# First products on row halves: seven products for eight in weighted groups 2 to 5 of an attention and routing kernel

## The chip, the cores and the metric

The kernel runs on one core of a Trainium2 chip. The metric is the device time of one execution in microseconds; several runs are taken, and their median counts. All data are 32-bit floats.

## The reference, cut to what matters

A sketched attention makes `x`, 4352 tokens of 128 numbers. Eight experts of two layers then work on every token, and their results are added with weights `P` that come from a balancing (Sinkhorn) loop over the gate's logits:

```python
for e in range(E):                      # 8 experts
    h = np.maximum(x @ w1[e], 0.0)      # 128 -> 1024, "first product"
    ye = h @ w2[e]                      # 1024 -> 128, "second product"
    out += P[:, e:e + 1] * ye
```

The weights are positive, so a token may be weighted before its first product as well as after its second.

## The kernel before, in words

**Groups, items, blocks.** The tokens are worked on in groups (line 632 on). Eight plain groups do experts 0 and 1 while attention and routing still run; their results wait in the tiles `kept`. Then come the weighted groups: five with three tiles of 256 tokens each (starts 1280, 512, 2048, 2816, 3584; these are "weighted groups 1 to 5"; the second does experts 2 to 7, the others 1 to 7), and a sixth with two tiles of 256. A pair of group and expert is an item. An item of a three-tile group has two blocks (`blocks`, line 882); a block holds four pieces `f` of 128 of the 1024 hidden numbers.

**One block of a three-tile group.** `four` (line 956) issues eight steps. A step is one first product (`first`, line 910): 128 rows of `x` against 128 columns of W1, as two matmuls in two column tiles of 64, for 512 or 256 tokens, into a fresh bank of the pool `aps` (four banks). ScalarE then writes the Relu of the bank into the block's buffer (`hx` for even blocks, `hb` for odd ones). VectorE makes the sums of hidden blocks that a fast second product needs (`sums`, ten instructions of 512 or 256 columns on lines 980 and 1000, from Relu results). Eight steps later `twenty` (line 1063) has the second products: ten pairs, each one product in each column tile, 128 rows, 256 tokens, added up in the four banks `s0` to `s3` over all experts of the group. Their weights are 16 sums of W2's blocks (`sums_of_four`, line 226) and four blocks of W2 as they are. GpSimd makes the 16 sums in group 1 with ten instructions an expert (line 242), SP stores them in DRAM, and groups 2 to 5 load them (line 230).

**Tokens and weights.** `prepare_x` (line 680) loads an item's weights `P` with a broadcasting DMA (line 674) and GpSimd multiplies the tokens by them (line 678), one item ahead. `prepare_w` (line 655) has SP load W1 and W2. `weigh_kept` (line 694) weighs the kept results of experts 0 and 1 on GpSimd.

**A group's end.** When a bank has its last product, `part_of_twenty` (line 814) copies it out on ScalarE and queues some 23 sums and 5 copies on half the partitions; then three transposes and the stores follow (`put`, line 711). They are taken one by one from the list `later` while the next group runs.

**What sets the order.** `steps` (line 1117) issues everything in program order, and TensorE and VectorE keep that order. `tc.keep_in_program_order` does the same for single instructions of GpSimd and SP. Elsewhere the framework orders ScalarE's, GpSimd's and SP's instructions. The two-tile groups go through `two` and `seven`: blocks of two pieces `f`, four steps, and seven second products, the last of which uses only one column tile. Waits between engines come from the framework, by what an instruction reads and writes.

## Time and profile before

| | us |
|---|---|
| median of 3 runs (919.47 to 919.66) | 919.57 |
| span of the profiled execution | 917.7 |
| DVE busy from 650 to 700 us | 30.93 |
| ACT busy from 650 to 700 us | 20.66 |

The profiled execution's span runs from its first to its last instruction; its own time as a run isn't listed apart, so the median, 1.9 us more, stands for it. PE is TensorE's matmuls, PEld its weight loads, DVE VectorE, ACT ScalarE, POOL GpSimd, SP the engine that issues most DMAs. A line such as "L916 PE MATMUL a<-xe,w 128\*64 128x512 f32 x1088 | 336.3, 592" names the line of the code, the engine, what is written and read, the weights' rows and columns, the result's partitions and columns, how many instructions there are, their busy time together and the mean time of one in ns. A product of 32-bit floats stands there as two matmuls, its two passes. A matmul's listed time includes a tail that the next one overlaps, so its rate is read from starts. In the table by stretches each line gives the stretch, its length, and the busy time and count of PE, PEld, DVE, ACT and POOL, then TensorE's granted clock, the DMA engines' busy share and GB/s. A square bracket in a timeline names what the engine waited for.

### The profile page before, as it was taken

What the parts mean: (1) busy time and instruction counts of PE and PEld (TensorE: products, weight loads), DVE (VectorE), ACT (ScalarE), POOL (GpSimd) and SP (SyncE); (2) the same over time, 40 slices, a digit from 0 to 9 for tenths busy, and PEclk for the clock granted to TensorE, in tenths of its full rate; (3) what the DMA queues carried; (4) which work ended last, traced back from release to release, by engine and by line L of the source; (5) the groups of instructions that cost most, each with busy time, mean ns of one, the idle gap of its engine ahead of it and who ended that gap; (6) DMA issues with size and microseconds to landing.
All of it is one profiled execution on the core that took longest, in us unless ns stands there. A gap on an engine that the chain in (4) does not pass through costs nothing.

```text
span 917.7 us, 18881 instructions
## 1 busy us (share of the span) xinstructions
PE 910.4 (99%) x7434; PEld 695.8 (76%) x7434; DVE 687.7 (75%) x1173; ACT 422.7 (46%) x918; POOL 210.4 (23%) x212
## 2 busy tenths in 40 slices
PE   9999999999999999999999999999999999999997
PEld 6777544466666688888888888888888888888997
DVE  7678699888876798766975666966667987678654
ACT  3355465554444454444544444544445444446443
POOL 3121100175545422200210011110100352340110
PEclk9999999999999999999999999999999999999999
DMA  9994100213445545534364343463434556552550
GB/s 250 307 276 165 54 1 1 70 64 110 161 142 152 172 133 158 182 110 146 115 173 148 110 150 110 122 200 120 140 113 165 148 161 190 164 192 92 150 158 13
DMA packets 91305, 128.15 MB, mean 140 GB/s; under 512 B 25392, under 2 KB 69504, under 8 KB 86480
## 3 DMA queue, kind: packets, MB, share of 16 engines
q1 hardware_dynamic: 88384, 121.42, 43.0%
q0 software_dynamic: 1600, 5.36, 2.0%
q8 instruction: 58, 0.95, 0.4%
q10 hardware_dynamic: 1232, 0.16, 0.1%
q14 instruction: 31, 0.25, 0.1%
HBM read 107.88 MB, written 19.05 MB: 138 GB/s over the span
## 4 chain that ended last, share of the span: by engine, by line
PE 96%; DVE 2%; ACT 1%; DMA 1%; issue 0%; SPq 0%; DVEq 0%; ACTq 0%
PE a L916 51%; PE s L1107 41%; PE a L347 1%; PE a L462 1%; DMA kx<-in_k_dram 1%; DVE hb L933 1%; PE a L314 0%; PE s L376 0%; PE a L426 0%; PE s L392 0%; DVE cs L602 0%; PE a L496 0%; PE a L392 0%; ACT hb L920 0%; DVE rs L596 0%
## 5 line engine op out<-in xcount | busy, mean ns | idle before, releaser
L916 PE MATMUL a<-xe,w 128*64 128x256 f32 (+1 forms) x2560 | 615.4, 470 | 0.0
L916 PEld LDWEIGHTS a<-xe,w 128*64 128x64 f32 x2560 | 306.3, 137 | 39.2 <-issue 1.6
L920 ACT ACTIVATE hb<-a 128x256 f32<-128x256 f32 (+4 forms) x408 | 195.1, 480 | 241.7 <-PE a L916 210.9
L1107 PE MATMUL s<-hb,ws 128*64 128x256 f32 (+3 forms) x1312 | 276.4, 395 | 0.2 <-DVE hb L933 0.2
L920 ACT ACTIVATE hx<-a 128x256 f32<-128x256 f32 (+1 forms) x360 | 167.3, 465 | 211.6 <-PE a L916 194.6
L1107 PE MATMUL s<-hx,ws 128*64 128x256 f32 x1280 | 253.6, 379 | 0.0
L1107 PEld LDWEIGHTS s<-hb,ws 128*64 128x64 f32 x1312 | 161.5, 137 | 67.9 <-issue 14.7
L980 DVE TENSOR_TENSOR hb<-hb 128x512 f32<-128x512 f32 (+1 forms) x204 | 138.3, 687 | 97.9 <-ACT hb L920 93.8
L678 POOL TENSOR_TENSOR xe<-xT,xe 128x768 f32<-128x768 f32 (+2 forms) x41 | 84.0, 2050 | 490.5 <-DMA xe<-pT 363.6
L1107 PEld LDWEIGHTS s<-hx,ws 128*64 128x64 f32 x1280 | 159.6, 137 | 48.3
L980 DVE TENSOR_TENSOR hx<-hx 128x512 f32<-128x512 f32 (+1 forms) x204 | 149.0, 741 | 59.1 <-ACT hx L920 54.1
L1107 PE MATMUL s<-hb,w 128*64 128x256 f32 (+3 forms) x536 | 120.3, 408 | 0.0
L916 PE MATMUL a<-xT,w 128*64 128x416 f32 (+3 forms) x512 | 119.9, 462 | 0.0
L1107 PE MATMUL s<-hx,w 128*64 128x256 f32 x384 | 81.8, 379 | 0.0
L933 DVE TENSOR_TENSOR hb<-hb 128x416 f32<-128x416 f32 (+7 forms) x84 | 59.9, 713 | 19.4 <-ACT hb L920 15.8
L1107 PEld LDWEIGHTS s<-hb,w 128*64 128x64 f32 x536 | 60.0, 137 | 17.4 <-issue 6.5
L916 PEld LDWEIGHTS a<-xT,w 128*64 128x64 f32 x512 | 49.5, 137 | 25.0 <-issue 15.6
L242 POOL TENSOR_TENSOR ws<-w 128x256 f32<-128x256 f32 (+1 forms) x70 | 61.1, 907 | 8.1 <-DMA w<-in_moe_w_dram 8.0
L933 DVE TENSOR_TENSOR hx<-hx 128x256 f32<-128x256 f32 (+1 forms) x65 | 37.2, 576 | 25.4 <-ACT hx L920 24.2
L1107 PEld LDWEIGHTS s<-hx,w 128*64 128x64 f32 x384 | 46.4, 137 | 4.4
L980 DVE TENSOR_TENSOR pqg<-hb 128x512 f32<-128x512 f32 x68 | 43.2, 676 | 0.0
L980 DVE TENSOR_TENSOR pqg<-hx 128x512 f32<-128x512 f32 x68 | 37.7, 594 | 0.0
(180 smaller groups left out, 489.8 us busy)
## 6 DMA issues: line engine op xcount, KB each, us to landing
w<-in_moe_w_dram SPq DMA_DIRECT2D x82, 512.0 KB, 5.5
ws<-ws SPq DMA_DIRECT2D x34, 1024.0 KB, 4.9
xe<-pT SPq DMA_DIRECT2D x34, 384.0 KB, 4.0
ws<-ws SPq DMA_DIRECT2D x12, 512.0 KB, 3.1
ph<-qa SPq DMA_DIRECT2D x12, 288.0 KB, 4.8
rb<-qb SPq DMA_DIRECT2D x3, 1152.0 KB, 7.6
pb<-pT SPq DMA_DIRECT2D x6, 384.0 KB, 8.6
kx<-in_k_dram SPq DMA_DIRECT2D x4, 544.0 KB, 5.0
```

What stands on the lines that cost most here:

```text
L242: tc.keep_in_program_order(nc.gpsimd.tensor_tensor(ws[:, c:c + len(ns)], blocks(x), blocks(y), op=Alu.subtract if off else Alu.add))
L347: nc.tensor.matmul(pv[64 * s:64 * (s + 1), i], kp[0:n, H * t + h].rearrange("p i j -> p (i j)"), vx[0:n, slots[h], t, :], start=(t == 0 an ...
L462: nc.tensor.matmul(pn[64 * s:64 * (s + 1), t, 2 * i:2 * i + 2].rearrange("p h d -> p (h d)"), ph[:, i, s, 64 * t:64 * (t + 1)], kvs[b % 2] ...
L678: tc.keep_in_program_order(nc.gpsimd.tensor_tensor(out, x, pb, op=Alu.mult))
L916: nc.tensor.matmul(ph[sl], loaded_w[j][0][:, P * f + H2 * s:P * f + H2 * (s + 1)], sources[j][:, lo:hi], start=True, stop=True, tile_posit ...
L920: nc.scalar.activation(out=out, in_=ph, func=Act.Relu)
L933: nc.vector.tensor_tensor(out, a, b, op=Alu.subtract)
L980: nc.vector.tensor_tensor(out if not isinstance(out, tuple) else places(*out), places(*a), places(*b) if isinstance(b, tuple) else b, op=A ...
L1107: nc.tensor.matmul(sums[g][i][H2 * s:H2 * (s + 1), n * place:n * (place + 1)], w, x, start=c == 1 and not seeded, stop=c == per, tile_posi ...
```

## The change

Weighted groups 2 to 5 get a new routine, `middle`, with an order of its own, and group 1 prepares what it needs.

- **The first product.** W1 and the tokens are cut in pieces: rows 0 to 63 and 64 to 127, and tokens 0 to 383 and 384 to 767 (`HALF` is 384). Two pieces `f` that lie two apart are taken together. A product of two by two blocks is then done with seven block products instead of eight, in Winograd's way: with sums of W1's pieces (`wf`, beside W1's own pieces in `wl`), and sums of the tokens' pieces (`de`, and the changed upper half of `xe`). Each of the seven is 64 rows, 128 columns (two column tiles) and 384 tokens; three or four in each half `p` of the block run in the upper 64 rows of the array and the others in the lower ones.
- **Sums of its results.** The four banks of `aps` become `bx`, `by`, `bb[0]` and `bb[1]`. In each half `p` of a block ScalarE copies product 1 from `bx` to `bb[p]` (`seed`), copies product 5 out (`m5`), and does four Relu of 384 columns; VectorE does two sums (`vector`) of a bank and the copied product 5, one of them into the bank `by`.
- **The second product** is cut into row halves as well, so that all matmuls have the same tiles: 20 pairs of 64 rows instead of 10 of 128. All 20 forms of W2 are now stored and loaded (16 before). Two row halves that add into the same bank are kept apart by waits: the second waits for an instruction of ScalarE or VectorE that saw a later first product (`witness`).
- **The tokens.** VectorE weighs half an item a block, ScalarE copies it, and four DMAs issued by GpSimd that add to their target make the token sums (`join_halves`).
- **W1's forms** are made once, in group 1 (`forms_of_first`): copies and sign changes by ScalarE, three adding DMAs an expert by GpSimd, stores by SP.
- **Group 6's** sums of W2 (`sums_of_two`) are made again by GpSimd instead of being loaded. `weigh_kept` goes in pieces of 256 columns.
- **Order.** Each instruction of a block has a time in a period of 8.83 us; the instructions are issued in the order of these times, blocks overlapping. At the start ten whole products of an older block are put in between, at the end three blocks of group 6.

```diff
+        def product(out, row, w, c0, x, start, stop):
+            r = ROWS[row]
+            for s in range(2):
+                sl = slice(H2 * s, H2 * (s + 1))
+                nc.tensor.matmul(out[sl], w[r, c0 + H2 * s:c0 + H2 * (s + 1)], x[r], start=start, stop=stop,
+                                 tile_position=(H2 * row, H2 * s), skip_group_check=True)
...
+            product(*{1: (bx, 0, w1, fa, xe[:, 0], True, False), 2: (bx, 1, w1, fa, xe[:, 0], False, True),
+                      3: (by, 1, w1, fb, de[:, 0], False, True), 4: (b, 1, wf, fb, xe[:, 1], False, True),
+                      5: (b, p, wf, fa, de[:, 1], True, False), 6: (b, 0, wf, fb, de[:, 0], False, True),
+                      7: (b, 0, w1, fb, xe[:, 1], False, True)}[n])
...
+        def scalar(k, p, what):
+            b = bb[p]
+            if what == "seed":
+                witness(k, p, 1, nc.scalar.copy(b, bx))
+            elif what == "m5":
+                witness(k, p, 5, nc.scalar.activation(out=m5s[p], in_=b, func=Act.Copy, scale=1.0 if p else -1.0))
+            else:
+                out, x = {"11": (raw(k, p, 0, 0), bx), "12": (raw(k, p, 1, 0), by), "21": (raw(k, p, 0, 1), b),
+                          "22": (raw(k, p, 1, 1), raw(k, p, 1, 1))}[what]
+                ins = nc.scalar.activation(out=out, in_=x, func=Act.Relu)
...
+        def vector(k, p, what):
+            ins = nc.vector.tensor_tensor(by if what == 1 else raw(k, p, 1, 1), bb[p], m5s[p], op=Alu.add)
...
+        FIRST = {1: (1.40, 5.39), 2: (3.85, 6.44), 3: (5.60, 10.11), 4: (6.61, 11.37), 5: (-0.07, 4.62), 6: (3.76, 6.34), 7: (5.60, 8.35)}
+        SCALAR = {"seed": (2.93, 5.41), "m5": (2.86, 5.40), "11": (4.03, 9.98), "12": (6.42, 11.91), "22": (11.16, 12.70), "21": (7.68, 12.16)}
+        VECTOR = {1: (5.46, 7.30), 2: (5.97, 8.48)}
+        SECOND = ((14.81, 12.90, 15.44, 15.42, 15.62, 19.89, 21.05, 20.44, 21.90, 22.30),
+                  (17.63, 17.59, 19.18, 21.80, 21.41, 23.38, 23.73, 22.41, 24.54, 24.29))
+        EASE, WEIGH = (11.93, 16.87, 13.85), 13.49
...
+        def second_product(k, i, row):
+            r = ROWS[row]
...
+                before = written.get((bank_, 1 - row))
+                op = None
+                if before is not None and bank_ not in waited[row]:
+                    op = next((op for seen, op in witnesses if seen > before), None)
...
+                mm = into(g, w[r], x[r], *place, row)
+                if op is not None:
+                    tc.add_manual_dep(mm.ins, op, SYNC, reason="row tiles of one bank")
...
+    SUMS = ((14.78, (U4, U2), (at(0, 0), at(3, 0)), (at(0, 1), at(3, 1)), False),
+            (11.17, (U1,), (at(3, 0),), (at(3, 2),), False), (13.68, (V4,), (U1,), (at(0, 2),), False),
+            (15.02, (V3, V1), (U4, U2), (at(1, 1), at(2, 1)), True),
+            (14.65, two_, (at(1, 1), at(3, 1)), (at(0, 1), at(2, 1)), True),
+            (16.68, pqg[:, 2], (V3,), (at(1, 0),), True),
+            (14.66, (BB, U3), (at(1, 2), at(2, 0)), (at(2, 2), at(2, 2)), False),
+            (19.10, (W1, W2), (V4, V4), two_, False), (16.15, (W3, V2), (BB, U3), (V1, at(1, 2)), False),
+            (20.68, (W4,), pqg[:, 2], (V2,), True))
...
+    def join_halves(j):
+
+        xe, de = sources[j]
+        for out, x in ((de[upper], xe[lower]), (de[lower, 1], xe[upper, 1]), (de[:, 0], de[:, 1]),
+                       (xe[lower, 1], xe[lower, 0])):
+            tc.keep_in_program_order(nc.gpsimd.dma_start(out=out, in_=x, accum_op=Alu.add))
...
+    def forms_of_first(e, w1):
...
+        def turn(out, x):
+            nc.scalar.activation(out=out, in_=x, func=Act.Copy, scale=-1.0)
+
+        def plus(out, x):
+            tc.keep_in_program_order(nc.gpsimd.dma_start(out=out, in_=x, accum_op=Alu.add))
...
+        def one():
+            nc.scalar.copy(d, w[:, :, 1])
+            turn(fa, w[:, :, 0])
+
+        def two_():
+            nc.scalar.copy(t3[lower], w[upper, :, 1])
+            turn(n12, w[lower, :, 1])
+            plus(a[:, 0:F // 2], a[:, F // 2:F])
+
+        def three():
+            turn(z[lower], w[upper, :, 1])
+            plus(b[lower, F // 2:F], less[lower])
+
+        def four_():
+            turn(z[upper], d[lower])
+            put_(wf[lower, :, 0], d[lower])
+            put_(wl[lower, :, 1], t3[lower])
+
+        def five():
+            plus(a[:, 0:F // 2], b[:, 0:F // 2])
+
+        def six():
+            put_(wf[upper, :, 0], z[upper])
+            put_(wf[:, :, 1], d)
+
+        return {2: one, 4: two_, 6: three, 8: four_, 12: five, 16: six}
...
+    PERIOD = 8.83
...
+        for n, i in enumerate((0, 1, 2, 5, 3, 4, 6, 7, 8, 9)):
+            add(0.2 + 0.8 * n, whole_product, ks[0] - 2, i)
```

The keys 2 to 16 of `forms_of_first` are steps of the item in group 1 (eight a block; 16 is the next item's first). In the tables the two numbers of `FIRST`, `SCALAR` and `VECTOR` are for the halves `p` = 0 and 1, the two rows of `SECOND` for the row halves, and `SUMS` lists VectorE's ten sums with their times.

More of the change, by code (lines that the diff above doesn't have):

```diff
@@ L185, with load_w @@
     load_q(0, 16)
-    def load_w(e, sums=True, again=False):
+    lower, upper = slice(0, H2), slice(H2, P)
+    def load_w(e, sums=True):
         w1 = wpool.tile([P, F], F32, tag="w1", name="w1")
@@ L571, in routing @@
     def routing():
+        for e in range(1, E):
+            raw_of_first(e)
         yield 5
@@ L625 @@
     engines = mybir.EngineType
-    lower, upper = slice(0, H2), slice(H2, P)
     NMAX = 512
@@ L835, in part_of_twenty @@
             do(y[lower, 1], y[lower, 1], own[1][lower, 1], True)
-        elif k == 3:
+        if all(i in own for i in range(4)):
             e0, e1, e2, e3 = (own[i] for i in range(4))
@@ L1098, in into @@
         seen = done[g]
-        c = seen[i, s] = seen.get((i, s), 0) + 1
-        per = len(es) * (FO // (4 if t == 3 else 2)) * TIMES[t][i][s]
+        c = seen[i, s] = seen.get((i, s), 0) + (2 if t == 3 and row is None else 1)
+        per = len(es) * (FO // (2 if t == 2 else 4)) * TIMES[t][i][s] * (2 if t == 3 else 1)
         if g in DIRECT:
@@ L1119, in steps, with between @@
         todo, sums_at, t = {}, {}, 0
-        for k in range(len(blocks) + 5):
+        ks = range(len(blocks) + 5)
+        news = [k for k in range(len(blocks)) if new_of(blocks[k][0])]
+        def between(t):
+            for do in sums_at.pop(t, ()):
+                do()
+            while soon:
+                soon.pop(0)()
+            for b, p in todo.pop(t, ()):
+                second(b, p)
+        for k in ks:
+            if k in news:
+                if k == news[0]:
+                    while todo or sums_at:
+                        between(t)
+                        t += 1
+                    with tc.manual_schedule(engines={engines.DVE, engines.PE, engines.Activation}):
+                        middle()
+                    yield 0
+                continue
             if k == len(blocks) - 2:
```

394 lines of the change are left out of this document (289 added, 105 removed).

## The prediction

> **What bounds the kernel now.** I read the page's busy shares first, then the chain that ended last, then the table by stretches of time.
>
> ```profile
> span 917.7 us, 18881 instructions
> PE 910.4 (99%) x7434; PEld 695.8 (76%) x7434; DVE 687.7 (75%) x1173; ACT 422.7 (46%) x918; POOL 210.4 (23%) x212
> PE 96%; DVE 2%; ACT 1%; DMA 1%; issue 0%; SPq 0%; DVEq 0%; ACTq 0%
> ```
>
> ```profile
> 250.00:300.00 50.00, 50.00 (x385) 33.20 (x383) 35.99 (x55) 20.68 (x43) 23.23 (x23) 1.00 0.49 151
> 650.00:700.00 50.00, 50.00 (x380) 40.34 (x378) 30.93 (x54) 20.66 (x43) 3.80 (x2) 1.00 0.44 140
> ```
>
> In both stretches of the weighted groups TensorE is busy 50.00 of 50.00 us at clock 1.00, and 96% of the chain lies on it. So a column less to stream is time won, until another engine becomes the bound. How long one column takes, and one block:
>
> ```profile
> 624.69 1.07 DVE L980 TENSOR_TENSOR hx<-hx 128x512 f32<-128x512 f32 x2 [0.71 <-ACT hx L920]
> 634.17 1.08 DVE L980 TENSOR_TENSOR hb<-hb 128x512 f32<-128x512 f32 x2 [0.71 <-ACT hb L920]
> ```
>
> ```profile
> 347.85 0.43 PE s L1107 x4
> 348.28 0.86 PE a L916 x4
> 349.14 0.43 PE s L1107 x4
> ```
>
> The first two lines (VectorE's timeline) are the first sum of two blocks that follow one another: a block takes 9.48 us. In the chain, four matmuls are one product in two column tiles, each in two passes: 0.43 us for 256 columns, 0.86 for 512, so 0.216 and 0.43 us a pass. A block has 4 first products of 512 columns, 4 of 256 and 10 pairs of second products of 256: 4 x 0.86 + 14 x 0.43 = 9.46 us. The block is TensorE's stream and nothing else.
>
> **The change, part by part.** *The stream of groups 2 to 5.* They hold 6 + 3 x 7 = 27 items of 2 blocks, 54 blocks. A first product on 128 rows becomes, in each half p of a block, seven products on 64 rows and 384 columns. Seven land in each row half of the array per block (p0: 5, 1, 6, 7 above, 2, 3, 4 below; p1: 1, 6, 7 above, 2, 3, 4, 5 below). The ten second products run once in each half. A tile then has 7 x 2 passes of 384 columns, 0.323 us each (between the rows for 256 and 512), and 20 of 0.216: 4.52 + 4.32 = 8.83 us. Against 9.48 that removes 0.645 us a block, **34.8 us** in 54.
>
> Do four tiles of 64 x 64 run at once? The trace has such tiles in the lower row half alone, never four. The nearest rows:
>
> ```profile
> 8.74 1.99 PE L376 MATMUL s<-qT,wq 64*128 64x512 f32 x8
> 10.66 2.33 PEld L347 LDWEIGHTS a<-v,kp 128*64 128x64 f32 x72 [0.76 <-PE s L376]
> 22.86 0.85 PE L376 MATMUL s<-qT,wq 64*128 64x288 f32 x4
> 23.65 0.65 PE L916 MATMUL a<-xT,w 128*64 128x256 f32 x4
> ```
>
> Eight passes of 512 columns in two row halves took 1.99 us; one after another would be 8 x 0.43 = 3.4. So row halves run side by side, as column halves do in every block. 72 weight loads, with as many matmuls among them, took 2.33 us: 32 ns a pair. The change issues 136 pairs a block, 65 ns each. I take full concurrency; the other end is two tiles at a time (a rival).
>
> And must a matmul wait for the one ahead of it in the program, though its tile is free? Around an odd product for one column tile (the seventh of `seven`):
>
> ```profile
> 863.51 0.38 PE L1107 MATMUL s<-hx,ws 128*64 128x256 f32 x1
> 863.65 0.38 PE L916 MATMUL a<-xe,w 128*64 128x256 f32 x1
> 863.73 0.38 PE L1107 MATMUL s<-hx,ws 128*64 128x256 f32 x1
> ```
>
> A product of the next step starts in the other tile between two passes of the odd one. A tile goes on by itself, at least one pass ahead. The Trainium skill (TensorE: Matmul & The Clock Gate, Part 3, The mechanism) says that matmuls start and end strictly in program order. By that rule the two passes of one tile would hold up the next tile, and two of four would run at a time (the rival's price); these rows speak against it.
>
> *VectorE.* It keeps its ten sums a block and gets four sums out of the banks and one weighing.
>
> ```profile
> 629.98 1.02 DVE L980 TENSOR_TENSOR pqg<-hx 128x512 f32<-128x512 f32 x2
> 630.91 0.69 DVE L980 TENSOR_TENSOR hx<-hx,pqg 128x512 f32<-128x512 f32 x1
> 631.52 1.48 DVE L980 TENSOR_TENSOR hx<-hx 128x512 f32<-128x512 f32 x2
> 636.11 0.42 DVE L980 TENSOR_TENSOR hb<-hb 128x256 f32<-128x256 f32 x1 [0.87 <-ACT hb L920]
> L477 DVE TENSOR_TENSOR rd<-a,rc 128x384 f32<-128x384 f32 x9 | 5.0, 558 | 0.3
> ```
>
> Back to back, 512 columns take 0.61 us from start to start (630.91 to 631.52) though each is listed with 0.69, and 512 with 256 behind it 0.93 (629.98 to 630.91), so 256 take 0.33. The last line is the nearest to the new sums, bank and tile, 384 columns: 0.558 listed, 0.47 by the same overlap. Sum: 6 x 0.61 + 4 x 0.33 + 5 x 0.47 = 7.3 us. To that come a finished group's 23 sums and 3 transposes, three pops a block over ten blocks: 0.9. **8.2 of 8.83 us**, or, if no overlap is had, 6 x 0.69 + 4 x 0.42 + 5 x 0.56 + 1.1 = 9.7. The order written out puts no sum behind the one that it needs, so I take the lower end; the upper is a rival.
>
> *The handoffs.* Product 7 waits for the sum v1, product 4 for v2; in between VectorE has three sums of 512 and v2, 3 x 0.61 + 0.56 = 2.4 us, and the lower row half has products 3 and 2 and two second products, 2 x 0.645 + 2 x 0.43 = 2.15. So v1 has to be 0.25 us early. Walking one block with these durations (a bank is ready 0.16 us after its stream, 0.38 less 0.216, and I allow 0.1 for the signal) I get v1 0.7 us early, v2 0.4, and VectorE 0.3 idle in the block. Each wait stands in TensorE's one queue, and a late one holds all four tiles. I book 0 and keep up to 0.3 us a block.
>
> *ScalarE* has 13 instructions a block where it had 8.
>
> ```profile
> L920 ACT ACTIVATE hb<-a 128x384 f32<-128x384 f32 x32 | 15.6, 493 | 16.0 <-PE a L916 11.4 <-PE s L1107 2.6 <-ACT hb L920 1.4
> L920 ACT ACTIVATE hx<-a 128x512 f32<-128x512 f32 x4 | 2.4, 599 | 2.3 <-PE a L916 2.3
> ```
>
> 13 x 0.49 = 6.4 of 8.83 us: hidden in the stream.
>
> *GpSimd and the queues in groups 2 to 5.* The weighing of an item leaves GpSimd; four adding DMAs an item come.
>
> ```profile
> 604.33 1.91 POOL L678 TENSOR_TENSOR kept<-kept,pb 128x768 f32<-128x768 f32 x1 [12.73 <-DMA pb<-pT]
> 626.63 1.09 DVE L980 TENSOR_TENSOR hx<-hx 128x256 f32<-128x256 f32 x1 [0.87 <-ACT hx L920]
> L488 POOL DMA_DIRECT2D xT<-xd x12: 550/550/577, 53.6 to 101.2; - x12
> DMA to landing us min/median/max: 1.9/3.1/7.9
> ```
>
> The adding DMAs are issued 20 us ahead of use. The longest dependent run is three; at 0.55 us to issue and 3.1 to land, twice that if adding doubles it, 11 to 20 us: hidden. SP loads two W1 forms and the 20 forms of W2 an item, 5 us each (below), 13 us ahead of use: hidden. What isn't hidden: the kept rows are still weighed on GpSimd, now in 25 pieces of 256 columns. A sum that ran beside GpSimd (626.63) took 1.09 us; its like at 636.11 took 0.42. 25 x up to 0.66 = 17 us of delay on VectorE, part of it inside the 0.3 to 0.7 of slack: **5 us** (0 to 17). The Trainium skill (SBUF — State Buffer, Who interferes with whom) has this as a rule: VectorE with two inputs in SBUF contends with a GpSimd instruction that reads SBUF. The four sums from a bank have one such input and would be spared by it; no run here shows that.
>
> *Into and out of the new stretch.* 10 whole products at its start and 12 steps of group 6 at its end use all 128 rows among the row halves. From the last row-half stream (22.86 + 0.85 less the 0.16 tail = 23.55) to 23.65 a change of form costs 0.1 us; up to 44 changes, 4.4 us, and the rows must be level: **6 us** (2 to 13).
>
> *Weighted group 1* makes the forms of W1 for seven experts.
>
> ```profile
> 300.38 7.78 POOL L242 TENSOR_TENSOR ws<-w 128x256 f32<-128x256 f32 x10 [2.80 <-DMA w<-in_moe_w_dram]
> 295.76 1.82 POOL L678 TENSOR_TENSOR xe<-xT,xe 128x768 f32<-128x768 f32 x1 [7.54 <-PE a L916]
> ws<-ws SPq DMA_DIRECT2D x34, 1024.0 KB, 4.9
> w<-in_moe_w_dram SPq DMA_DIRECT2D x82, 512.0 KB, 5.5
> ```
>
> Per expert ScalarE gets six passes of 512 columns and two copies of 256, 6 x 0.6 + 0.8 = 4.4 us; it is busy 20.68 of 50 above, so its idle time hides them. GpSimd has 7.8 + 1.8 us of 19 and gets three issues, 1.7 us. But ScalarE's fourth step reads what an adding DMA made, and that DMA stands behind the ten adds in GpSimd's queue; SP's stores wait likewise, and the next expert's loads stand behind them. **4 us** (0 to 35, the upper end 5 us each for seven).
>
> **The sum.** 34.8 less 5 + 6 + 4 is 19.8 us: a span of 898 from 917.7. The median shown, 919.57, is 1.9 above that span; I predict **900 us**.
>
> **The rivals.**
> 1. *TensorE waits at the handoffs* for 0.25 us a block more: 54 x 0.25 = 13.5, 913. For it: slack of 0.3 to 0.7 us on waits in one queue. Against: 0 idle now.
> 2. *VectorE becomes the bound*, and the kernel slower. At 9.7 us in the three quarters of the blocks that carry a group's ends, and 8.83 otherwise, the mean is 9.48, so nothing is won; with the 15 us booked above, 919.6 + 15 = 935. It decides from a block of 9.48 - 15 / 54 = 9.2 us on. For it: 8.2 of 8.83 with every overlap had, and two sums a block that wait for a bank. Against: the 0.61 us cadence holds wherever sums stand back to back.
> 3. *Group 1 holds ScalarE* behind an adding DMA, 5 us an expert: 31 more than booked, 931. Against: idle time on either side.
> 4. *The four tiles don't run at once*: 17.7 us a block, 919.6 + 54 x 8.2 = 1362. Against: rows 8.74 and 863.65.
>
> **Chances.** Forecast 0.53 (its own range 887 to 909), rival 1 0.20, rival 2 0.17, rival 3 0.07, rival 4 0.03. Within 0.2% (1.8 us, about what a measurement of this kernel can tell from no change) I put 0.01 of rival 1 and 0.02 of rival 2. Faster: 0.53 + 0.19 = 0.72; slower: 0.15 + 0.07 + 0.03 = 0.25. The range takes in rivals 1 and 3 and the lower part of rival 2: 887 to 933.
>
> **What would show it.** Right: a block of 8.83 to 8.95 us between first sums, TensorE busy in all of it, VectorE 85 to 95%. Rival 1: gaps on TensorE released by VectorE or ScalarE in each block. Rival 2: VectorE without idle time, TensorE's gaps released by line `vector`. Rival 3: gaps of TensorE in the stretch of 190 to 330 us, with ScalarE waiting for a DMA. The prediction is wrong if the block is over 9.2 us, or if the ends cost more than the 15 us booked.

## The result, and the profile after

The changed kernel takes **998.05 us** (median of 4 runs, 994.06 to 1002.6) against 919.62 (919.47 to 920.16) on the same chip: a ratio of 1.0853, 95% interval 1.082 to 1.0886. Forecast were 900, and 887 to 933 as the range. The profiled execution has a span of 997.8 us, 80.1 more than before.

The page of the changed kernel: span, busy shares, the granted clock in 40 slices of 25 us, and the chain that ended last.

```profile
span 997.8 us, 26767 instructions
PE 923.4 (93%) x10934; PEld 606.1 (61%) x10934; DVE 775.2 (78%) x1438; ACT 549.8 (55%) x1248; POOL 266.6 (27%) x336
PEclk9999999979988786899999999999999999999999
PE 70%; DMA 13%; POOL 6%; DVE 4%; issue 4%; ACT 2%; SPq 1%; POOLq 0%; DVEq 0%; ACTq 0%
```

TensorE's share of the chain has gone from 96% to 70%, and 13% are on DMAs. The clock row says where: the digits below 9 stand in slices 9 to 17, some 200 to 420 us. The table by stretches (busy us of each engine in 100 us, then granted clock, DMA share, GB/s) tells the same:

```profile
185.00:285.00 100.00, 73.47 (x490) 38.55 (x488) 53.81 (x75) 40.66 (x86) 45.91 (x54) 0.85 0.50 141
285.00:385.00 100.00, 72.88 (x474) 35.62 (x472) 51.93 (x72) 41.48 (x87) 44.60 (x48) 0.85 0.53 137
500.00:600.00 100.00, 98.59 (x1490) 71.80 (x1486) 93.31 (x191) 66.69 (x151) 19.55 (x23) 1.00 0.69 195
700.00:800.00 100.00, 97.61 (x1474) 69.02 (x1470) 89.31 (x183) 65.08 (x147) 17.73 (x22) 1.00 0.71 198
```

The first two rows are weighted group 1: TensorE works 73 of 100 us, at clock 0.85, and no engine is near its limit. The last two are the new stretch: TensorE 98, VectorE 89 to 93.

I cut the run at three starts: the first weighted product on 128 rows, the first on 64 rows (the new stretch), and the first of group 6. Group 1 took 133.3 us before and **199.4** after (185.1 to 384.5): 66.1 more. The new stretch took 511.8 and 514.5, the rest 87.7 and 98.8. So five sixths of the loss lie in the group that only *prepares* the new stretch, and the new stretch itself gained nothing. (It also holds the ten whole products that group 1 still did before, 10 x 0.43 = 4.3 us; group 1 alone did that much less work and still took longer.) How an expert of group 1 goes, in the timeline of all engines (the bracket is the idle time ahead, and what ended it):

```profile
287.50 2.03 POOL L754 TENSOR_TENSOR px<-xT,px 128x768 f32<-128x768 f32 x1 [2.99 <-DMA px<-pT]
289.50 8.33 POOL L240 TENSOR_TENSOR ws<-w 128x256 f32<-128x256 f32 x10
297.86 0.33 SPq L247 DMA_DIRECT2D ws<-ws  x1
298.24 0.52 SPq L281 DMA_DIRECT2D wf<-wb  x1
298.85 1.33 SPq L281 DMA_DIRECT2D wf<-wa  x1
304.06 0.62 ACT L284 COPY wa<-w 128x512 f32<-128x512 f32 x1 [10.02 <-DMA wf<-wb]
305.50 0.85 POOL L278 DMA_DIRECT2D wa<-wa  x1 [7.67 <-ACT wa L275]
306.70 1.12 PE L1035 MATMUL a<-px,w 128*64 128x256 f32 x4 [7.49 <-ACT hb L1039]
307.60 1.07 PE L1408 MATMUL s<-hb,ws 128*64 128x256 f32 x4
308.46 1.77 PE L1035 MATMUL a<-px,w 128*64 128x512 f32 x4
309.63 0.63 ACT L275 ACTIVATE wb<-wa 64x512 f32<-64x512 f32 x1 [2.03 <-DMA wa<-wa]
```

GpSimd weighs when the weights have landed, then does its ten adds for W2's forms. SP's store of these (L247) waits for them, and the last stores of the *previous* expert's W1 forms (L281) stand behind it in SP's queue. They free the room into which ScalarE makes the next expert's first form, and ScalarE waits for that 10.02 us with all evictions behind it. TensorE then stands still for 7.49 us, and the passes behind the gap are slow: four of 256 columns take 0.86 us from start to start (307.60 to 308.46), twice the 0.43 that they take in the kernel before, and the four of 512 columns at 308.46 are listed with 1.77 us. The like at full clock, at 310.49 in the same timeline, are listed with

```profile
310.49 1.02 PE L1035 MATMUL a<-px,w 128*64 128x512 f32 x4
```

That agrees with the Trainium skill (TensorE: Matmul & The Clock Gate, Part 1, What's actually happening): after an idle window the array runs at half its clock. The waits from 185 to 400 us (engine, line, what it waited for: us in all, times, longest), SP's queue in the second block:

```profile
PEld a L1035 <- ACT hb L1039: 58.6, 10, 13.8
ACT wa L284 <- DMA wf<-wb: 48.0, 5, 11.4
POOL wa L278 <- ACT wa L275: 32.5, 5, 7.7
ACT wb L275 <- DMA wa<-wa: 25.3, 7, 14.3
```

```profile
SPq L247 <- POOL ws L240: 79.6, 7, 14.4
SPq L281 <- DMA wa<-wa: 32.1, 7, 8.1
```

TensorE waits for ScalarE, ScalarE for a store, SP for GpSimd, and GpSimd for ScalarE: a circle through four queues, once per expert.

In the new stretch the period itself is as forecast. VectorE's first sum of four blocks that follow one another:

```profile
865.35 0.57 DVE L1256 TENSOR_TENSOR a<-a,hb 128x384 f32<-128x384 f32 x1 [0.24 <-ACT hb L1251]
874.18 0.57 DVE L1256 TENSOR_TENSOR a<-a,hb 128x384 f32<-128x384 f32 x1 [0.81 <-ACT hx L1251]
883.02 0.57 DVE L1256 TENSOR_TENSOR a<-a,hb 128x384 f32<-128x384 f32 x1 [1.14 <-ACT hb L1251]
891.85 0.57 DVE L1256 TENSOR_TENSOR a<-a,hb 128x384 f32<-128x384 f32 x1 [0.59 <-ACT hx L1251]
```

8.83, 8.84 and 8.83 us; so is the median of all 53 periods. Their sum is 493.2, though, against 53 x 8.83 = 468.0. The 25 us over are at the start (the first two of these sums stand at 398.62 and 415.58, 16.96 apart), some 4 at each of three changes of group, 1.4 and 2.3 in two blocks where VectorE's weighing waits for its weights, and 2.0 in a block where one VectorE sum lasts 3.10 us beside GpSimd's weighing of kept rows. Some 10 us more go ahead of the first of these sums: 14.1 us pass from the first 64-row product to it, for 3.8 us of stream, and the granted clock there is 0.62. At a change of group ScalarE's copy of a bank stands ahead of evictions and waits for TensorE's last product; the late weights stand behind 16 output stores in SP's queue:

```profile
522.88 0.59 ACT L940 COPY z<-s 128x512 f32<-128x512 f32 x1 [1.23 <-PE s L1408]
```

```profile
608.86 12.86 SPq L994 DMA_DIRECT2D out_dram<-yt  x16
621.76 0.48 SPq L750 DMA_DIRECT2D px<-pT  x1
```

The long sum, in VectorE's and GpSimd's timelines:

```profile
464.67 3.10 DVE L1121 TENSOR_TENSOR hb<-hb 128x512 f32<-128x512 f32 x1
465.14 3.20 POOL L822 TENSOR_TENSOR kept<-kept,kept 128x256 f32<-128x256 f32 x3
```

At the end some 8 us more go where 64-row products and 128-row products of group 6 wait for each other.

### The profile page after: what moved, and what is told of

Its sections match the earlier page's. It is cut to its first block, busy times and chain, and to the rows that moved or that the text cites. A ratio compares the mean times of both kernels' runs of the same rounds, so it can differ in the third digit from the quotient of the medians.

```text
span 997.8 us, 26767 instructions
## 1 busy us (share of the span) xinstructions
PE 923.4 (93%) x10934; PEld 606.1 (61%) x10934; DVE 775.2 (78%) x1438; ACT 549.8 (55%) x1248; POOL 266.6 (27%) x336
## 4 chain that ended last, share of the span: by engine, by line
PE 70%; DMA 13%; POOL 6%; DVE 4%; issue 4%; ACT 2%; SPq 1%; POOLq 0%; DVEq 0%; ACTq 0%
PE s L1408 30%; PE a L1219 25%; PE a L1035 11%; POOL ws L240 5%; DMA wf<-wb 3%; DMA wb<-less 2%; DMA px<-pT 2%; DMA wa<-wb 1%; DVE hb L1121 1%; DMA wa<-wa 1%; PE a L408 1%; DMA w<-wf 1%; DMA de<-de 1%; PE a L523 1%; SPq L994 1%
## 5 line engine op out<-in xcount | busy, mean ns | idle before, releaser
L1408 PE MATMUL s<-hb,ws 64*64 64x256 f32 (+4 forms) x2704 | 367.1, 389 | 1.8 <-DVE hb L1121 1.6
L1219 PE MATMUL a<-xe,w 64*64 64x384 f32 x1732 | 339.5, 489 | 2.4 <-ACT hx L1251 2.4
L1408 PE MATMUL s<-hx,ws 64*64 64x256 f32 (+1 forms) x2632 | 341.4, 381 | 0.4 <-DVE hx L1121 0.4
L1219 PE MATMUL a<-de,w 64*64 64x384 f32 x1296 | 254.0, 488 | 8.1 <-issue 2.8
L1408 PEld LDWEIGHTS s<-hb,ws 64*64 64x64 f32 (+1 forms) x2704 | 187.6, 135 | 98.0 <-issue 49.8
L1408 PEld LDWEIGHTS s<-hx,ws 64*64 64x64 f32 (+1 forms) x2632 | 181.6, 134 | 75.5 <-issue 28.4
L1035 PE MATMUL a<-px,w 128*64 128x256 f32 (+1 forms) x832 | 175.1, 468 | 53.9 <-ACT hb L1039 53.6
L1219 PEld LDWEIGHTS a<-xe,w 64*64 64x64 f32 x1732 | 116.0, 133 | 31.4 <-ACT hx L1251 5.1
L1251 ACT ACTIVATE hb<-a 128x384 f32<-128x384 f32 x162 | 77.1, 492 | 47.5 <-PE a L1219 44.8
L1039 ACT ACTIVATE hx<-a 128x256 f32<-128x256 f32 (+1 forms) x144 | 58.8, 422 | 51.4 <-PE a L1035 48.4
L1247 ACT ACTIVATE hb<-a 128x384 f32<-128x384 f32 x108 | 53.0, 491 | 34.8 <-PE a L1219 33.8
```

What stands on the lines that cost most here:

```text
L1035: nc.tensor.matmul(ph[sl], loaded_w[j][0][:, P * f + H2 * s:P * f + H2 * (s + 1)], sources[j][:, lo:hi], start=True, stop=True, tile_posit ...
L1039: last_relu[:] = [nc.scalar.activation(out=out, in_=ph, func=Act.Relu).ins.name]
L1219: nc.tensor.matmul(out[sl], w[r, c0 + H2 * s:c0 + H2 * (s + 1)], x[r], start=start, stop=stop, tile_position=(H2 * row, H2 * s), skip_grou ...
L1247: witness(k, p, 5, nc.scalar.activation(out=m5s[p], in_=b, func=Act.Copy, scale=1.0 if p else -1.0))
L1251: ins = nc.scalar.activation(out=out, in_=x, func=Act.Relu)
L1408: mm = nc.tensor.matmul(sums[g][i][H2 * s:H2 * (s + 1), n * place:n * (place + 1)], w, x, start=c == (2 if t == 3 and row is None else 1) ...
```

## The experiments

Theory A at first: one wait, for the adding DMAs and the stores behind them, costs the time in group 1. Its rival: the loss is the circle of queues, in which every wait mended is followed by the next. The table cuts each run as above (us; "rest" from group 6's first product to the end of the span; before beside it: 133.3, 511.8, 87.7). The change, c1, c2, c4, c6 and c7 are medians of 4 to 12 runs; every other time is a single run. e4 stands on e3, and beyond these four most kernels stack the edits of earlier ones.

| run | time | before on that chip | group 1 | new stretch | rest |
|---|---|---|---|---|---|
| the change | 998.05 | 919.62 | 199.4 | 514.5 | 98.8 |
| e1_no_forms | 943.26 | 918.83 | 148.6 | 507.2 | 98.5 |
| e2_six_early | 1002.55 | 918.83 | 215.8 | 501.3 | 98.9 |
| e3_adds_late | 986.84 | 918.83 | 192.7 | 508.7 | 98.8 |
| e4_reordered | 981.58 | 918.83 | 186.1 | 509.8 | 98.8 |
| p2_gpsimd_forms | 977.88 | 919.93 | 185.5 | 507.4 | 98.8 |
| m1_no_forms_eased | 922.55 | 919.93 | 145.0 | 490.5 | 98.9 |
| a1_all | 958.72 | 919.93 | 183.4 | 489.5 | 99.0 |
| b1_reordered_gpsimd | 933.57 | 918.42 | 158.0 | 490.6 | 98.9 |
| b2_reordered_no_forms | 915.03 | 918.42 | 135.6 | 491.0 | 98.8 |
| b3_reordered_adding_dmas | 962.42 | 918.42 | 186.4 | 490.1 | 99.0 |
| c1_reordered_again | 930.47 | 919.5 | 153.5 | 490.2 | 99.0 |
| c2_scalar_by_hand | 928.25 | 919.57 | 136.9 | 504.3 | 99.4 |
| d1_only_scalar_by_hand | 1018.94 | 919.57 | 218.7 | 514.2 | 99.2 |
| d2_adds_late_by_hand | 966.33 | 919.57 | 169.2 | 512.1 | 98.9 |
| c4_start_early | 925.08 | 918.91 | 147.6 | 490.4 | 99.4 |
| c5_same_adding_dmas | 919.35 | 918.91 | 143.7 | 490.6 | 99.0 |
| c6_copies_later | 923.81 | 919.11 | 152.1 | 490.2 | 99.0 |
| c7_tail_grouped | 920.77 | 919.11 | 148.9 | 493.0 | 95.8 |

### One edit at a time

**e1_no_forms**: W1 is written whole into both arrays, and its forms are left out.

```diff
-        return {2: one, 4: two_, 6: three, 8: four_, 12: five, 16: six}
+        return {16: lambda: None}
```

> Leaves out the forms of W1 (both stored tiles are W1 as it is, so the first products of groups 2 to 5 use other weights); everything else as in the changed kernel. All theories that blame the making of the forms: group 1, 199 us long in the changed kernel and 133 before, comes back to 133 to 138, and the whole takes 925 to 935. The rival that blames something else in group 1 (the two copies of W2's blocks an expert, the order of the second products, the lower clock by itself): group 1 stays over 180, the whole over 980.

943.26, between the two: the forms cost 55 of the 78 us, and 24 are lost without them. Group 1 still takes 15 us more than before, 12.5 of them in its last block of some 22 us. ScalarE's timeline there:

```profile
319.29 0.51 ACT L798 COPY de<-xe 128x384 f32<-128x384 f32 x1 [9.06 <-POOL xe L789]
333.62 0.51 ACT L798 COPY de<-xe 128x384 f32<-128x384 f32 x1 [9.00 <-POOL xe L789]
```

Twice ScalarE waits 9 us for GpSimd's weighing of the new stretch's first tokens. This is a second cause, apart from the forms.

**e2_six_early**: the last stores of an expert's forms one step ahead of the next expert's store.

```diff
+        return {2: one, 4: two_, 6: three, 8: four_, 12: five, 15: six, 16: lambda: None}
```

> Step six of an expert's forms (two stores) moves from the next item's step 0 to step 15 of its own item, so that SP has it ahead of the next store of W2's forms, which waits for GpSimd's ten adds. Theory A (ScalarE's step one waits for these stores, 10 us an expert): nearly all of the 66 us in group 1 comes back, whole 935 to 945. Theory B (the wait only hides the next one: ScalarE's step four needs the first adding DMA, which stands behind the ten adds in GpSimd's queue): the wait moves to step four, group 1 stays over 165, whole 960 to 998.

1002.55: no gain, and slower than both theories allowed; ScalarE's 48.0 us at L284 became 23.1, and its 25.3 at L275 (behind an adding DMA) became 82.6. The single wait of theory A fell, and the loss stayed.

**e3_adds_late**: the ten adds of the next expert and their store at step 10 of the item instead of ahead of step 0. **e4_reordered**: that, and the steps 2, 4, 6, 8, 9 and 13.

```diff
+                    if c + 8 * q == 10 and items[j + 1][0] == PLAIN:
+                        second_forms(j + 1)
```

> The ten adds of the next expert's W2 forms (and their store) move from step 0 to step 10 of the item, behind the first two adding DMAs in GpSimd's queue; the forms' steps stay. Theory A: step six is now ahead of that store in SP's queue, so its wait is gone, 935 to 945. Theory B: the wait at step four goes too, but the third adding DMA (step 12) stands behind the adds, so step six lands late and step one still waits some 5 us an expert: group 1 about 165, whole 955 to 970.

> Adds at step 10 as in the run before, and the forms' steps at 2, 4, 6, 8, 9 (five) and 13 (six), so that all three adding DMAs are ahead of the adds and the stores ahead of the next item. Both theories: no queue holds ScalarE, group 1 133 to 142 us, whole 928 to 940. If the forms' own work on ScalarE or the traffic were the cause, it would stay near 998.

986.84 and 981.58: both missed. Theory A is dropped; whichever link was moved, most of the loss stayed, as a circle would have it.

### Two places, taken apart

**p2_gpsimd_forms** (on e3's order, with the forms at steps 1, 2, 3, 5, 7 and 9): `plus` as a GpSimd operation on the words instead of an adding DMA. **m1_no_forms_eased** (on e1): four edits around the new stretch. **a1_all**: both, with the forms made.

```diff
-            tc.keep_in_program_order(nc.gpsimd.dma_start(out=out, in_=x, accum_op=Alu.add))
+            tc.keep_in_program_order(nc.gpsimd.tensor_tensor(out, x, y, op=Alu.subtract if off else Alu.add))
...
-                    add(t + WEIGH - 9, fetch_weights, ahead)
+                    add(t + WEIGH - 18, fetch_weights, ahead)
...
+            for n, a in enumerate(ends):
+                heapq.heappush(jobs, (at_ + 1.5, 10 ** 6 + next(count_), lambda a=a: part(*a)))
```

> W1's forms as three GpSimd operations on the words in place of three adding DMAs (and three ScalarE operations fewer per expert); the ten adds for W2's forms stand behind them, at step 10 instead of step 0. Theory A (what cost weighted group 1 its time is the latency of the chain ScalarE, adding DMA, ScalarE, adding DMA, store, 5 to 14 us for each link): with GpSimd's links of about 2 us an item takes 20 to 21 us instead of 29 and the time falls from 998 to 940 to 955. Theory B (GpSimd, SP and the DMA engines have too little room in group 1, whatever makes the forms): GpSimd's work only grows, and the time stays at 970 to 990, by the 982 of the run with adding DMAs in the same order.

> No forms are made (W1 is written whole into both arrays, so this run leaves the making of the forms out, as the first experiment did: 943). On top of it four edits around groups 2 to 5: the first new item's weights are fetched earlier; its adding DMAs are issued in two parts so that the second item's weighing does not wait behind them; weights in the middle are fetched one block earlier; the copies of a finished group's banks stand 1.5 us later in ScalarE's program. Theory A (the 24 us that the run without forms lost against before are waits at the edges of the new stretch: about 20 at its start, 9 at three changes of group, 5 behind output stores): 912 to 922. Theory B (the edges are slow because the transfers are slow or the array's two shapes do not overlap there): 935 to 943.

> All of the edits of the two runs before, with the forms made (full computation). Theory A: the sum of both, 915 to 930. Theory B (GpSimd, which then has weighing, forms and adding DMAs in one queue, becomes the bound in group 1 or at the start): 945 to 975.

p2 has theory B's size, 977.88: without a single adding DMA for the forms, group 1 is as long as in e4. m1, half a microsecond above theory A's range, took 17 us off the new stretch (507.2 to 490.5): the first block of each of the three changes of group came from 11.5 us to 9.1, and the first 64-row products reach VectorE's first sum in 5.7 us instead of 10.1. But the wait for the first tokens stayed: group 1 still takes 11.7 us more than before. a1, with both, has theory B's size, 958.72: the stretch keeps m1's gain, and group 1 is as long as in p2. SP's, GpSimd's and ScalarE's timelines of m1 there:

```profile
306.85 0.32 SPq L248 DMA_DIRECT2D ws<-ws  x1
307.22 0.42 SPq L751 DMA_DIRECT2D px<-pT  x1
```

```profile
314.95 0.99 POOL L790 TENSOR_TENSOR xe<-xT,px 128x384 f32<-128x384 f32 x1 [8.13 <-DMA px<-pT]
```

```profile
315.97 0.51 ACT L799 COPY de<-xe 128x384 f32<-128x384 f32 x1 [14.35 <-POOL xe L790]
```

The weights are fetched in the instant the store of W2's forms lets SP go, land 7.7 us later, and ScalarE has waited 14.35 us. The ten adds seem to hold the start through SP's queue, as they hold each expert; b1 and b2 put that to the test.

### The order of the queues

**b1_reordered_gpsimd**: on SP the next expert's loads first and the store of W2's forms two steps into the next expert; on GpSimd W1's forms, then the weighing, then the ten adds. **b2_reordered_no_forms**: that order without the forms (left out). **b3_reordered_adding_dmas**: that order with the adding DMAs.

```diff
-        nc.sync.dma_start(out=stored_four[e], in_=ws)
+        stores.append(lambda: tc.keep_in_program_order(nc.sync.dma_start(out=stored_four[e], in_=ws)))
...
+                    if c + 8 * q == 2:
+                        while stores:
+                            stores.pop(0)()
+                    if c + 8 * q == 8:
+                        while weighings:
+                            weighings.pop(0)()
```

> As a1_all (959), full computation, with the queues of weighted group 1 put in another order: the next expert's loads and weights go out on SP first, the store of W2's forms two steps into the next expert instead of ahead of its loads; on GpSimd W1's forms come first, then the weighing of the next expert's tokens, then the ten adds; the weighing of the kept sums comes last. Theory A (what is left in group 1 is a circle through SP's and GpSimd's queues: ten adds, their store, the next weights' load behind it, 7 to 8 us of landing, the weighing, the forms behind that, ScalarE behind the forms): the circle is opened and group 1 takes 135 to 145 us instead of 183; 908 to 922 in all. Theory B (GpSimd's own work, now 16 of 19 us an expert with forms, is the bound of the group): group 1 stays above 165 us and the time above 940.

> The same order without W1's forms (left out, as in m1_no_forms_eased: 922). Theory A (the 17 us lost at the start of the new stretch there come from the weights of its first tokens landing at 314.7, behind the store of W2's forms at 306.6): with the store behind the load they go, 905 to 912. Theory B (the start is lost to the two shapes of tile side by side and to the chain of adding DMAs): 916 to 924.

> As b1_reordered_gpsimd, full computation, but with the adding DMAs and ScalarE's copies of the change as they are, at steps 2, 4, 6, 8, 9 and 13. Theory A (the order of the queues, not the adding DMAs, cost the time): within 8 us of b1_reordered_gpsimd. Theory B (each adding DMA of 4 to 8 us holds ScalarE): 15 to 40 us above it.

Group 1 went from 183.4 to 158.0 in b1, 25 us where theory A had 38 to 48, and 933.57 lies between the two theories. Without forms (b2) it is 135.6, 2 over before, and ScalarE's longest wait for the first tokens there is 6.6 us instead of 14.3; the whole, 915.03, is a microsecond from theory B's range all the same, because the new stretch didn't get shorter (491.0 for m1's 490.5). That kernel is 3.4 us *faster* than before: so little the change is worth (in a single run) when its preparation costs nothing and the edges stay. b3 is 28.9 us above b1, theory B as it seemed then.

### ScalarE's order

**c1_reordered_again** moved steps once more (ten adds at 12, the last forms at 9, 11 and 13, weights of both first items earlier). **c2_scalar_by_hand** keeps ScalarE in written order from the second expert on; **d1_only_scalar_by_hand** and **d2_adds_late_by_hand** do so on the change and on e3's order.

```diff
+                if j == first_weighted + 1 and q == 0:
+                    by_hand.enter_context(tc.manual_schedule(engines={engines.Activation}))
```

> As b1_reordered_gpsimd (934), full computation, with three places changed that its trace showed: ScalarE's and GpSimd's last forms at steps 9, 11 and 13 and the ten adds behind them at 12 (they wait for the array until about step 10, and ScalarE waited up to 6 us for the forms behind them); a fourth room for weights, so that the weights of both first new items are fetched in the expert before (the second landed at 333, behind the loads of W1's forms). Theory A (these are waits in queues, 12 us in the second expert, 4 at its followers, 8 at the start): 910 to 920. Theory B (in the second expert one VectorE instruction of 10.1 us ran just as long as GpSimd worked without a break; if GpSimd at work is what holds VectorE, another order of the same GpSimd work keeps that loss): 922 to 932.

> As c1_reordered_again (930), full computation, with ScalarE kept in the order in which the program is written from the second expert of weighted group 1 on; there the compiler's scheduler had put the fourth form's ScalarE operation three evictions behind the second's instead of eight, and ScalarE waited 30 us in all for GpSimd in front of it. Theory A (the place in ScalarE's order is the cause of what is left in group 1): the 30 us of waits go, of which 12 to 15 stood on the path: 914 to 920. Theory B (the circle is GpSimd's: ten adds that wait for their room, then forms): ScalarE waits elsewhere, 926 to 932.

> The change as it is, full computation, and one edit: ScalarE in written order from the second expert of weighted group 1 on. If the scheduler's places for ScalarE's operations were the cause of the 66 us in group 1 (theory A), 940 to 960. If it is the chain of adding DMAs behind the ten adds (theory B), the waits stay where they are or move by a few steps: 980 to 1000.

> As d1_only_scalar_by_hand, with the ten adds at step 10 behind the first two adding DMAs, and the steps of the forms spread (1, 2, 3, 9, 10 and 15), so that ScalarE asks for the first adding DMA's result seven steps, 8 us, after its issue. Theory A: 935 to 950. Theory B: the weights' load and GpSimd's weighing behind the store still delay the first forms: 965 to 985, by the 982 of e4_reordered.

c1: 930.47 (ratio 1.0124, 1.0107 to 1.0141), theory B's size, but not for its reason: no VectorE instruction of its profile ran over 3.42 us. c2: 928.25 (1.009, 1.0054 to 1.0125); its total is B's, its group 1 is A's: 136.9 us with the forms made, 3.6 more than before. Two waits of c1 in group 1 that are no longer among c2's longest:

```profile
ACT wb L274 <- POOL wa L277: 30.1, 5, 7.5
PEld a L1040 <- ACT hb L1044: 15.7, 5, 5.0
```

A form's step in the program hadn't set its place on ScalarE: b1 has the last of ScalarE's forms at step 5 and c1 at step 9, and in the timelines of both it stands two evictions behind the form ahead of it; in written order (c2) seven lie between. But the written order alone, on the change (d1), is slower still at 1018.94, outside both expectations, and d2, with the ten adds and the steps moved too, takes 966.33, theory B's size: in these runs ScalarE's order helped only where the other queues were in order too. c2's gain in group 1 was lost at once at the new stretch's start, 14 us longer, with its first adding DMAs for the tokens now too late (TensorE's timeline of c2; c4 tests it):

```profile
332.74 0.90 PE L1224 MATMUL a<-de,w 64*64 64x384 f32 x2 [3.22 <-DMA de<-de]
```

### The start, the adding DMAs, the end

**c4_start_early**: the first new item weighed, copied and half joined one expert earlier, ahead of the ten adds. **c5_same_adding_dmas**: the same with W1's forms as in the change, by ScalarE and adding DMAs. **c6_copies_later** and **c7_tail_grouped**: c5 with the second item's copies four steps later and the first item's weighing one step earlier; and c6 with group 6's early steps in three groups.

```diff
+        elif c in (9, 10):
+            weigh_half(j, c - 9, nc.gpsimd)
+        elif c == 12:
+            copy_half(j, 0)
+            copy_half(j, 1)
+            join_halves(j, 0)
...
-                add(t + 4.6 * n + 1 + 1.15 * c, step_of_two, k, c)
+                add(t + 4.6 * n + 4.2 + 0.05 * c, step_of_two, k, c)
```

> As c2_scalar_by_hand (928), full computation; the only edit: the first new item is weighed, copied and its first two adding DMAs issued one expert earlier (ahead of the last ten adds), the second item in the place where the first stood. In c2 group 1 took 137 us, 3 more than before, and 19 us of TensorE's time were lost at the start of the new stretch, where its third product waited for the adding DMA that landed at 332.7, 11 us after the stretch began. Theory A (the chain of two pairs of adding DMAs, 8 us each, behind the ten adds sets the start): 8 to 14 us go, 913 to 920. Theory B (the start is lost to the two shapes of tile that wait for each other): 924 to 929.

> As c4_start_early, full computation, but W1's forms made as in the change, by ScalarE and adding DMAs (at steps 1, 2, 3, 9, 10 and 15). It prices the adding DMAs alone with everything else mended. Theory A (order is what counts, and an adding DMA with 7 steps until its result is asked for costs nothing): within 5 us of c4_start_early. Theory B (their landing, 4 to 8 us and more when the queues are busy, still holds ScalarE): 10 to 30 us above it.

> As c5_same_adding_dmas (919, level with before), full computation, adding DMAs kept; ScalarE's copies of the second new item four steps later (its trace shows ScalarE 4.9 us behind GpSimd's weighing there, and TensorE idle for 2.5 us behind ScalarE), the first item's weighing one step earlier, ahead of the third adding DMA. Theory A (what is left at the start is ScalarE's place behind GpSimd): 914 to 917. Theory B (it is the change of tile shape and VectorE behind GpSimd): 918 to 921.

> As c6_copies_later, and at the end of the new stretch the four steps of each of the three 128-row blocks that run early are issued together, in three groups instead of twelve single steps between 64-row products. Some 8 us of TensorE's time are lost there, where each 128-row product waits until both halves of its rows are free. Theory A (each change of shape costs, so fewer changes cost less): 3 to 5 us below c6_copies_later. Theory B (the loss is that the last products of the two halves follow one another, whatever stands between them): within 1.5 us of it.

c4: 925.08 (1.0066, 1.0052 to 1.0079), B's size, but the stretch did gain 14 us as A said, and group 1 lost 11 of them (below). c5: 919.35, level with before (one run). **The same adding DMAs that went with 998 go with 919.** With seven steps between the first one's issue and its use they cost no more than GpSimd's operations on the words do in c4. b3, at 962, had four steps there and ScalarE in the scheduler's order; which of the two cost it more was not taken apart. c6 and c7 spread: 916.72 to 929.91 and 917.43 to 927.79 over 12 runs each, where before has 918.25 to 922.33; medians 923.81 (1.0045, 1.0022 to 1.0069) and 920.77 (1.0027, 1.0005 to 1.0049). No version is shown to beat the kernel before. c5's one run lies within the spread of these two, so 919 is not its time to the microsecond. c6 missed both expectations. c7's median is 3 us below c6's, theory A's size, but within the spread; in the profiles the stretch and the rest together take 588.8 us in c7 and 589.2 in c6, so the grouping gained nothing (theory B), and the difference lies in group 1. In the middle of c5's stretch TensorE is the bound again (its table by stretches):

```profile
400.00:500.00 100.00, 99.98 (x1528) 77.69 (x1522) 95.50 (x195) 68.75 (x157) 23.71 (x27) 1.00 0.68 190
```

What is left in group 1 then, VectorE's and GpSimd's timelines of c4 (window 303 to 320) and c5 (219 to 233):

```profile
305.34 12.22 DVE L1126 TENSOR_TENSOR hb<-hb 128x512 f32<-128x512 f32 x1
```

```profile
305.47 6.39 POOL L241 TENSOR_TENSOR ws<-w 128x256 f32<-128x256 f32 x10
311.25 1.83 POOL L277 TENSOR_TENSOR wa<-w 128x512 f32<-128x512 f32 x1
312.45 1.47 POOL L810 DMA_DIRECT2D de<-de  x1
313.61 2.45 POOL L277 TENSOR_TENSOR wb<-wb,w 64x512 f32<-64x512 f32 x1
315.78 2.61 POOL L793 TENSOR_TENSOR xe<-hb,px 128x384 f32<-128x384 f32 x1
```

```profile
222.04 8.97 DVE L1131 TENSOR_TENSOR hb<-hb 128x512 f32<-128x512 f32 x1
```

```profile
222.37 6.04 POOL L241 TENSOR_TENSOR ws<-w 128x256 f32<-128x256 f32 x10
228.14 2.31 POOL L758 TENSOR_TENSOR kept<-kept,hb 128x256 f32<-128x256 f32 x3
```

A sum that takes 0.69 us elsewhere lasts 12.22 and 8.97 us, about as long as GpSimd works without a break (some of its instructions are left out above), and GpSimd's adds are quicker meanwhile (6.04 and 6.39 us for ten, 8.33 in the change). In c4 group 1 falls 10 us behind the kernel before just there. In c5 five experts have such a sum, of 5.7 to 9.0 us.

## Why the prediction was wrong, step by step

- **The failed step: weighted group 1**, booked at 4 us (0 to 35). It took 66.1. The prediction named the links (the fourth form behind an adding DMA behind the ten adds, SP's stores and the next loads behind them) and then priced it as one wait of 5 us per expert that idle time hides. It is a circle: each late link makes the next expert's first link later, so an expert took 28.5 us instead of 19. ScalarE's idle time (20.68 of 50 busy) was the wrong view; what counts is what stands in its queue ahead of the evictions. Rival 3 had the waits, with 7% and 931 us, but not that they add up. The clock, for which the sum had no term, added its part: at 0.85 TensorE is listed as busy for 146 of the 200 us, where group 1's columns at the prediction's pass times come to 129, so by this estimate some 17 of the 66 us. e1 (no forms: 55 us less, 51 of them in group 1) and c5 (the same operations in another order: 79 less, 56 of them in group 1) show that the forms and their order made it.
- **The stream: right.** Periods of 8.83, and counted by the columns of the matmuls in the trace, at the prediction's pass times and from group 1's first product on, TensorE's work fell from 728.0 to 693.1 us, 34.9 less (34.8 were forecast). The four tiles run at once; in the changed kernel's timeline four passes of 256 columns, two in each row half, take little more than one (0.38):

```profile
701.28 0.40 PE L1408 MATMUL s<-hx,ws 64*64 64x256 f32 x4
```

  The prediction drew the fourth rival's estimate, 1362 us, from the strict program order of the Trainium skill (TensorE: Matmul & The Clock Gate, Part 3, The mechanism); the period rules that out here.
- **VectorE: right.** 89 to 93 of 100 busy in the stretch, as the prediction's 85 to 95, and not the bound. **Handoffs: right at 0** in steady blocks: in the middle of c5's stretch TensorE is idle for 0.02 of 100 us.
- **ScalarE and the queues in the stretch: wrong in the ends of groups.** They were called hidden; the copies of finished banks and the 16 stores ahead of the weights cost some 17 us with the start's share, as m1 shows by taking them out.
- **Into and out: too small.** 6 us (2 to 13) were booked. In the change the start alone is 18 us over (10 ahead of the first sum, and 16.96 for 8.83), and the wait for its tokens reaches back into group 1's last block, for 12.5 in e1. With all mended (c5) some 19 remain: 2 ahead of the first sum, 3 in a first block of 12.1 us, 6 spread over the other periods, and 8 at the end.
- **GpSimd's pieces, 5 us (0 to 17):** not taken apart by a run. In the changed kernel's stretch one block is 2.0 us over where a sum of 0.69 us lasts 3.10 beside them; elsewhere in the stretch no VectorE sum lasts over 1.8 us. The larger effect of GpSimd on VectorE showed in group 1 of later runs, up to 12.2 us in one sum.
- **The balance, in c5:** group 1 is 10.4 us longer than before, the stretch and the rest together 9.9 shorter (589.6 for 599.5). The 34.9 us of stream are there; 25 of them don't show in the stretch and the rest (some 19 at its edges and changes of group, and 4.3 are the ten products that came over from group 1), and 10 go in its preparation.

## What to carry to other kernels

Preparation made "beside" a bound engine is priced by its queues, not by busy shares: draw each engine's queue for one turn, and see whether the last link of one turn stands ahead of the first of the next; if so, every latency in the circle is paid once per turn, and mending one link moves the wait. A step in the program is sure to set the order only on engines whose order is written by hand; read the order that the others got before pricing it. And a stretch with a period of its own pays at both ends and at each change within: count these edges against its length.

## What the runs showed of the hardware

- A VectorE sum that takes 0.69 us elsewhere lasted up to 12.2 us while GpSimd's instructions followed one another. The Trainium skill (SBUF — State Buffer, SBUF: two separate sides) has the two share a port pair by an exclusive lock held for a whole instruction; here, if it is this lock, VectorE did not get its turn between instructions for ten and more of them. That it is the cause is argued from the times alone. In the changed kernel's group 1 and in b2 the ten adds ran too, and no sum of group 1 took over 2.1 us; what makes the difference was not tried. It may also be why c6 and c7 spread by 13 and 10 us; that stays open.
- GpSimd's issue of an adding DMA took 0.99 us in the mean of 54 in the changed kernel, where plain issues, of 96 to 576 KB, took 0.55 to 0.64 before. That the adding makes the difference wasn't tested apart. The group of instructions (busy us, mean ns of one, idle time ahead):

```profile
L805 POOL DMA_DIRECT2D de<-xe x54 | 45.4, 990 | 216.3 <-PE a L1219 103.8
```
